# One core, an mLSTM cell into a SwiGLU block: weight pieces requested in pairs, a state sum moved, and one request placed between two halves of q's tiles

## The chip, the core and the metric

The kernel runs on one NeuronCore of one Trainium2 chip. The core has a matrix engine (TensorE, "PE" in the profile, with its weight loads as "PEld"), a vector engine (VectorE, "DVE"), a scalar engine for activations (ScalarE, "ACT"), a general engine (GpSimd, "POOL") and SyncE ("SP"), which here only issues transfers. Transfers are issued by SP and by ACT, each onto a queue of its own ("SPq", "ACTq"), and are carried out by 16 DMA engines that both queues share. Each engine runs its own instructions strictly in order, and waits on semaphores for the others.

The metric is device microseconds from start to end of one execution. The kernel before took 554.17 us (median of three runs, 553.81 to 554.72).

## What is computed

The reference has two stages. For 4 batches, 8 heads (32 sequences), 768 steps and a head width of 40, an mLSTM cell keeps a 40x40 state C, a normaliser n and a running maximum m per sequence:

```
m_new  = max(f_gate[t] + m, i_gate[t])
f_stab = exp(f_gate[t] + m - m_new);  i_stab = exp(i_gate[t] - m_new)
C = f_stab * C + i_stab * outer(v[t], k[t]);   n = f_stab * n + i_stab * k[t]
y[t] = sigmoid(o_gate[t]) * (C @ q[t]) / max(|n . q[t]|, 1)
```

The heads are put side by side, which gives x of 3072 tokens by 320, and

```
g = x @ w_gate            # 320 x 1536
h = g * sigmoid(g) * (x @ w_val)
out = h @ w_out           # 1536 x 320
```

The weights of the second stage come as float64. q, k, v and the gates are float32.

## The kernel before

**Tiling.** The 768 steps are cut into six groups of 128 tokens (`NG`), each for all 32 sequences, and each group into two chunks of 64. Within a group the cell is computed in its parallel form: scores of q and k, weights from the gates, the values weighed with them, and the state carried from chunk to chunk. The 32 sequences are handled in two halves, P = 0 and P = 1, of 16 sequences each. A group's output, 512 tokens in transposed form, then goes through the second stage in 12 blocks of 128 hidden features (`hidden(g, m)`: ten products per block, five for the gate and five for the value; the profile counts each float32 product twice, so twenty), and through w_out (`project`).

**Order.** The kernel is written out in program order by hand: what stands in the source is the order of each engine's queue. The first group has code of its own (the `first_...` functions, lines 478 to 562, called in lines 564 to 611). From then on the cell of group g+1 is computed in between the blocks of group g: `slots[m]` is a list of calls that come after `hidden(0, m)`, `ahead[m]` lists the weight blocks that are converted inside it, and `after[m]` does the same for the first group's product with w_out.

**Weights.** A float64 piece is brought in as raw 32-bit words by `piece_load(p)`. Pieces 0 and 1 hold one block of 128 features of w_gate and w_val each, pieces 2 to 6 two blocks each (piece 2 holds blocks 2 and 3, piece 3 blocks 4 and 5, and so on), and pieces 7 to 9 four row blocks of w_out each (converted as blocks 12 to 17). The gate half of a piece lands on partitions 0 to 63 and is issued by SP; the value half lands on partitions 64 to 127 and is issued by ACT for pieces 0 to 4, by SP for the rest. The raw words go to a home given by the caller (`h_sb` or `wo_sb`, which are not yet in use by then, or parts of them) or to one of two `raw` buffers, which is free again when both blocks of the piece that was in it have been scaled.

A block j is converted in three steps: `scale(j)`, two activations on ACT (`top`, line 190, and `low`, line 192); `join(j)`, two VectorE instructions that put the words together (lines 199 and 200); and `rounded(j)`, an addition of the low part (line 207) on GpSimd unless an engine is given. There is one `top` buffer and there are two `low` buffers. `hidden(0, j)` cannot start before block j is rounded.

**Psum.** There are four banks under the tag "cell" and four under "gen"; each `hidden` takes two "gen" banks and frees them when ACT (line 653) and VectorE (line 654) have read them.

**Around the change.** `first_state(P)` sums k and weighed v into the state for half P (16 small products, counted as 32) and copies it out. `first_seam(P)` transposes the group's output for the second stage. `burn(n)` runs n products of a constant tile, whose result nobody reads. `weights_load`, `weights_sub`, `weights_mask` and `weights_exp` make the weights of the next group (`w_sb`) from row maxima that pass through DRAM (`M_dram`); `weigh_values` makes `vw_sb` from them, which `do_add` needs. `load_squares` brings q's tiles of 32 by 32 with 16 small requests, eight for each parity of the head.

**Lanes.** Transfers share eight semaphores in turn, so each request waits until the request eight before it has landed.

Of the kernel before, what the change touches and what calls it, by code (L numbers as in the profile page):

```python
# [13 lines left out]
AF = mybir.ActivationFunctionType  # L14
# [10 lines left out]
def kernel(  # L25
# [18 lines left out]
    nc = tc.nc  # L44
# [7 lines left out]
    D1 = D + 1  # L52
# [4 lines left out]
    NKC = DM // HP  # L57
    UH = BH // 2
    UA = UH // 2
    NH = NFC + 1  # L60
# [15 lines left out]
    def bank(name, tag="cell"):  # L76
        return psum.tile([128, 512], F32, name=name, tag=tag)

    def half(i):
        return slice(i * SUB, (i + 1) * SUB)  # L80
# [5 lines left out]
    def heads(P):  # L86
        return slice(P * UH, (P + 1) * UH)

    k_sb = const.tile([128, BH, DP], F32)
    q_sb = const.tile([128, BH, DP], F32)  # L90
# [10 lines left out]
    wo_sb = const.tile([128, NFC, DM], F32)  # L101
    h_sb = const.tile([128, NH, TW], F32)
# [16 lines left out]
    def copy(eng, dst, src):  # L119
        if eng is nc.scalar:  # L120
            nc.scalar.copy(dst, src)
        else:
            eng.tensor_copy(dst, src)
# [16 lines left out]
    def piece_load(p, home=None):  # L140
        kind, m, n = PIECES[p]
        if kind == "gv":
            a, d = NKC, n * 128
            src = [(slice(i * HP, (i + 1) * HP), w[:, m * 128:(m + n) * 128].rearrange("(c p) f -> p c f", p=HP))
                   for i, w in enumerate((moe_w_gate, moe_w_val))]
            queues = (nc.sync, nc.scalar if p < 5 else nc.sync)
        else:
            a, d = n, DM
            src = [(slice(0, 128), moe_w_out[m * 128:(m + n) * 128].rearrange("(a p) d -> p a d", p=128))]
            queues = (nc.sync,)  # L150
        if src[0][1].dtype == F32:
            for r, w in src:
                if kind == "o":
                    nc.sync.dma_start(out=wo_sb[r, m:m + n, :], in_=w)
                else:
                    for x in range(n):
                        nc.sync.dma_start(out=wgv_sb[r, m + x], in_=w[:, :, ts(x, 128)])
            return
        if home is None:
            raw = conv.tile([128, 4 * NKC * 128], U32, name="raw")  # L160
        else:
            raw = home.rearrange("p a t -> p (a t)").bitcast(U32)
        raw = raw[:, 0:2 * a * d]
        for (r, w), queue in zip(src, queues):
            queue.dma_start(out=raw[r].rearrange("p (a d) -> p a d", a=a), in_=w.bitcast(U32))
        words = raw.rearrange("p (a d two) -> p a d two", two=2, a=a)
        raws[p] = (words[:, :, :, 0], words[:, :, :, 1])
        split(p)
# [35 lines left out]
    def rounded(j, eng=None):  # L204
        if j in blocks:
            lo, dst = blocks.pop(j)
            (eng or nc.gpsimd).tensor_tensor(dst, dst, lo, op=ALU.add)  # L207

    def convert(j, eng=None):
        scale(j)  # L210
        join(j)
        rounded(j, eng)
# [10 lines left out]
    warm = early.tile([128, 1], F32)  # L223
# [35 lines left out]
    step1 = keep1  # L259
# [46 lines left out]

    SQ = 32

    def load_squares(dst, a, c):
        for two in range(2):  # L310
            for s in range(2):
                r = slice((2 * two + s) * SQ, (2 * two + s + 1) * SQ)
                w = min(SQ, D - s * SQ)
                for t in range(L // SQ):
                    nc.sync.dma_start(out=dst[r, :, t, 0:w],
                                      in_=a[:, two:H:2, ds(c * L + t * SQ, SQ), ds(s * SQ, w)].rearrange("b h p d -> p (b h) d"))
# [6 lines left out]
    q_sq = q_sb.rearrange("p (a x) d -> p a (x d)", x=2).rearrange("p a (t d) -> p a t d", d=SQ)  # L323
# [17 lines left out]
        eng.tensor_tensor(vw_sb[:, heads(P)], v_sb[:, heads(P)], w_sb[:, heads(P), last].to_broadcast([128, UH, D1]),  # L341
                          op=ALU.mult)

    def small(name, n=UA):
        return bank(name)[:, 0:n * D1].rearrange("p (a d) -> p a d", d=D1)

    def add(n, P):
        ps = [small("add") for _ in range(2)]
# [8 lines left out]
    def state(s):  # L357
        return C_ring[s % 3]
# [103 lines left out]
    def sig(P):  # L462
        nc.scalar.activation(o_sb[:, heads(P)], o_sb[:, heads(P)], AF.Sigmoid)


    def burn(n, tag="cell"):
        t = bank("burn", tag)
        for _ in range(n):
            nc.tensor.matmul(t, lhsT=junk[:, 0:128], rhs=junk, start=True, stop=True)
# [4 lines left out]
    A, V, G = nc.scalar, nc.vector, nc.gpsimd  # L474
# [52 lines left out]
    def first_own(u):  # L527
        first_y[u] = bank("first_y", "gen")[:, 0:H * D1].rearrange("p (h d) -> p h d", d=D1)
        for h in range(H):
            nc.tensor.matmul(first_y[u][:, h, :], lhsT=W0[:, u * H + h, :], rhs=v_sb[:, u * H + h, :], start=True, stop=True)  # L530
# [13 lines left out]
            nc.vector.tensor_tensor(x, x, o_sb[:, u * H:(u + 1) * H], op=ALU.mult)  # L544
        nc.gpsimd.tensor_copy(x_sb[:, 2 * P:2 * P + 2, DM:], x_sb[:, 2 * P:2 * P + 2, 0:HP])

    def first_state(P, eng):
        ps = small("add")
        for a in range(UA):
            for two in range(2):  # L550
                h = P * UH + 2 * a + two
                nc.tensor.matmul(ps[half(two), a, :], lhsT=k_sb[:, h, :], rhs=vw_sb[:, h, :], start=True, stop=True)
        copy(eng, state(2)[:, P * UA:(P + 1) * UA], ps)

    def first_seam(P, engs):
# [30 lines left out]
    first_scores(1)  # L586
    first_x(1)
    sig(0)
    sig(1)
    piece_load(2, h_sb[:, NH - NKC:])  # L590
    piece_load(3, wo_sb)
    burn(3)
    first_own(2)
    first_own(3)
    first_gate(0)
    first_x(2)
# [1 line left out]
    first_seam(0, (A, A, V))  # L598
    scale(0)
    first_gate(1)  # L600
    burn(6, "gen")
    piece_load(4)
    join(0)
    first_seam(1, (A, A, V))
    rounded(0, V)
    first_state(0, A)
    late_decay()
    convert(1)
    nc.scalar.activation(step1, step1, AF.Exp)
    piece_load(5)  # L610
    nc.sync.dma_start(out=M_dram, in_=flat(M_sb))

# [104 lines left out]
    def load_all(dst, a, n):  # L717
        for P in range(2):
            load(dst, a, n, P)

    run = lambda f, *a: (lambda: f(*a))


    on_vector = (9, 10, 11)
    ahead = {m: [m + 2] for m in range(4)}
    ahead.update({4: [6], 5: [7, 8], 6: [9], 7: [10], 8: [11], 9: [], 10: [], 11: []})
    slots = {
        0: [run(first_state, 1, A), run(load_all, k_sb, k, 1), run(load_all, q_sb, q, 1)],
        1: [run(piece_load, 6, h_sb[:, NH - NKC:]), run(decay_rows)],
        2: [run(late_turns), run(weights_load, 1), run(load_all, v_sb, v, 1)],  # L730
        3: [run(decay)],
        5: [run(turn, 0, (A, A), (A, V))],
        6: [run(turn, 1, (A, A), (A, V)), run(weights_sub, 1, 0), run(weights_mask, 0), run(piece_load, 7)],
        7: [run(weights_sub, 1, 1), run(weights_mask, 1), run(nc.gpsimd.memset, q_sb, 0.0)],
        8: [run(weights_exp, 0), run(weights_exp, 1), run(weigh_values, G, 0), run(weigh_values, G, 1),
            run(piece_load, 8)],
        9: [run(do_scores), run(do_weigh, 0), run(do_weigh, 1), run(do_decayed, 2), run(load_all, o_sb, o_gate, 1)],
        10: [run(do_add, 1), run(do_state, 2), run(rounded, 12), run(load_squares, q_sq, q, 2)],
        11: [run(do_attend, 1, 0), run(do_gather, 1, 0, False), run(piece_load, 9)],
    }  # L740
    for m in range(NFC):
        first = [run(convert, j, V if j in on_vector else None) for j in ahead[m]]
# [34 lines left out]
    for g in range(1, NG):  # L777
        n, f = g + 1, g + 2
# [67 lines left out]
```

## Time and profile before

| | us |
|---|---|
| median of three runs | 554.17 (553.81 to 554.72) |
| the profiled execution | 555.16 |
| its span, first to last instruction | 553.0 |
| PE busy | 546.4 |
| DVE busy | 234.4 |
| ACT busy | 134.7 |
| POOL busy | 106.6 |

The span is the time from the first to the last instruction of the profiled execution; the 2.16 us beside it lie around it. All points in time given below are microseconds from the start of this span. In a timeline, a row gives the start, the duration of the whole run of like instructions, the engine, the line, and in brackets how long the engine was idle before and what ended that. The chain of waits is followed back from the last instruction: each row is what released the next one. In a table of stretches, the three numbers at the end are the granted TensorE clock (1.00 is full), the busy share of the DMA engines and the GB/s that they moved. A run of products has its end modelled, so that a row's start to the next row's start is the better measure of what it occupies.

### The profile page before, as it was taken

The numbers are of one execution on the slowest core, as the hardware profiler recorded it, in microseconds if no ns is written. First come the engines' busy times: TensorE is split into PE (matmuls) and PEld (weight loads), VectorE is DVE, ScalarE is ACT, GpSimd is POOL, SyncE is SP. The second block draws the span as 40 slices with busy tenths as digits, with TensorE's granted clock in tenths as the row PEclk, the third lists the DMA queues.
The fourth block names the chain that finished last, engine by engine and source line by source line (L and its number), as shares of the span: only waits on it lengthen the run. The fifth ranks groups of instructions, "written<-read, shape, count | busy, mean of one in ns | idle before, by whom it ended". The sixth has DMA issues, their size and how long they took to land.

```text
span 553.0 us, 11595 instructions
## 1 busy us (share of the span) xinstructions
PE 546.4 (99%) x4992; PEld 312.9 (57%) x4992; DVE 234.4 (42%) x394; ACT 134.7 (24%) x202; POOL 106.6 (19%) x97
## 2 busy tenths in 40 slices
PE   8999999999999999999999999999999999999997
PEld 4955546675545575544576455466455567444475
DVE  5956687962156332445521445531426621011100
ACT  4366564443101033110124101005110100111100
POOL 2314355574011151011133001114001200000000
PEclk9999999999999999999999999999999999999999
DMA  9999996798631763660464451395000131000000
GB/s 125 177 280 187 192 274 115 155 111 125 68 49 17 108 109 83 71 76 5 82 127 104 53 68 27 49 149 107 13 1 2 29 62 43 12 1 0 2 24 24
DMA packets 223994, 45.69 MB, mean 83 GB/s; under 512 B 214504, under 2 KB 219112, under 8 KB 223944
## 3 DMA queue, kind: packets, MB, share of 16 engines
q1 hardware_dynamic: 222036, 42.11, 46.7%
q10 hardware_dynamic: 1908, 2.85, 2.0%
q8 instruction: 39, 0.64, 0.5%
q14 instruction: 11, 0.09, 0.1%
HBM read 35.68 MB, written 4.01 MB: 72 GB/s over the span
## 4 chain that ended last, share of the span: by engine, by line
PE 92%; DMA 4%; SPq 3%; POOL 0%; DVE 0%; ACT 0%; issue 0%; ACTq 0%; POOLq 0%
PE gv_ps L648 55%; PE o_ps L664 24%; PE o_ps L671 5%; SPq L117 3%; DMA h_sb<-in_moe_w_val_dram 2%; PE inter L377 2%; PE sp L331 2%; PE intra L382 2%; DMA o_sb<-in_o_gate_dram 2%; PE add L353 1%; PE tp_kq L296 0%; POOL wgv_sb L207 0%; PE tp_x L439 0%; DVE wgv_sb L200 0%; ACT top L190 0%
## 5 line engine op out<-in xcount | busy, mean ns | idle before, releaser
L648 PE MATMUL gv_ps<-xT,wgv_sb 64*128 64x512 f32 x1440 | 317.3, 593 | 1.6 <-POOL wgv_sb L207 1.1
L648 PEld LDWEIGHTS gv_ps<-xT,wgv_sb 64*128 64x128 f32 x1440 | 139.1, 187 | 159.4 <-issue 154.6
L654 DVE TENSOR_TENSOR h_sb<-sg,gv_ps 128x512 f32<-128x512 f32 x72 | 49.5, 687 | 214.5 <-ACT sg L653 214.4
L664 PE MATMUL o_ps<-wo_sb,h_sb 128*128 128x320 f32 x480 | 130.5, 433 | 0.0
L664 PEld LDWEIGHTS o_ps<-wo_sb,h_sb 128*128 128x128 f32 x480 | 90.8, 190 | 41.0 <-issue 3.8
L653 ACT ACTIVATE sg<-gv_ps 128x512 f32<-128x512 f32 x72 | 43.0, 597 | 268.6 <-PE gv_ps L648 268.5
L362 POOL TENSOR_TENSOR C<-C,dec 128x328 f32<-128x328 f32 x20 | 14.5, 735 | 137.7 <-DVE C L369 137.6
L456 POOL TENSOR_SCALAR_AFFINE_SELECT w_sb<-w_sb 64x1024 f32<-64x1024 f32 x20 | 27.8, 1388 | 60.2 <-DVE w_sb L451 59.3
L658 ACT COPY z_sb<-o_ps 128x320 f32<-128x320 f32 x24 | 10.0, 422 | 94.7 <-PE o_ps L664 90.9
L403 POOL TENSOR_TENSOR o_sb<-o_sb,y_sb 128x640 f32<-128x640 f32 x10 | 14.3, 1428 | 79.2 <-DVE y_sb L394 79.1
L671 PE MATMUL o_ps<-wo_sb,h_sb 128*128 128x320 f32 x96 | 26.9, 437 | 0.0
L451 DVE TENSOR_TENSOR w_sb<-g_T,w_sb 128x1024 f32<-128x1024 f32 x10 | 13.2, 1355 | 27.6 <-DMA w_sb<-M_dram 27.6
L426 DVE STREAM_TRANSPOSE xT<-x_sq 128x640 f32<-128x640 f32 x16 | 12.5, 822 | 23.7 <-DMA x_sq<-x_sb 23.7
L671 PEld LDWEIGHTS o_ps<-wo_sb,h_sb 128*128 128x128 f32 x96 | 17.9, 190 | 7.2
L394 DVE TENSOR_TENSOR y_sb<-y_sb,intra 64x328 f32<-64x328 f32 x40 | 19.7, 493 | 0.8 <-PE intra L382 0.2
L369 DVE TENSOR_TENSOR C<-C,add 40x328 f32<-40x328 f32 (+1 forms) x36 | 17.7, 493 | 1.3 <-PE add L353 0.4
L207 POOL TENSOR_TENSOR wgv_sb<-wgv_sb,low 128x640 int32<-128x640 int32 x8 | 12.3, 1541 | 23.7 <-DVE wgv_sb L200 21.9
L377 PEld LDWEIGHTS inter<-C,qT 64*64 64x64 f32 x640 | 10.2, 134 | 7.3 <-issue 6.1
L341 POOL TENSOR_TENSOR vw_sb<-v_sb,w_sb 128x656 f32<-128x656 f32 x10 | 12.8, 1303 | 0.4
L338 DVE TENSOR_TENSOR w_sb<-sp,w_sb 128x512 f32<-128x512 f32 x20 | 12.7, 682 | 0.0
L460 ACT ACTIVATE w_sb<-w_sb 128x1024 f32<-128x1024 f32 x10 | 10.6, 1058 | 8.8 <-POOL w_sb L456 8.8
L397 DVE TENSOR_SCALAR den<-den 128x16 f32<-128x16 f32 x10 | 12.2, 1216 | 0.3
(129 smaller groups left out, 343.7 us busy)
## 6 DMA issues: line engine op xcount, KB each, us to landing
w_sb<-M_dram SPq DMA_DIRECT2D x10, 512.0 KB, 7.2
x_sq<-x_sb SPq DMA_DIRECT2D x128, 40.0 KB, 2.0
k_sb<-in_k_dram SPq DMA_DIRECT2D x12, 320.0 KB, 6.1
v_sb<-in_v_dram SPq DMA_DIRECT2D x12, 320.0 KB, 5.7
o_sb<-in_o_gate_dram SPq DMA_DIRECT2D x12, 320.0 KB, 5.4
raw<-in_moe_w_out_dram SPq DMA_DIRECT2D x3, 1280.0 KB, 7.8
out_dram<-z_sb SPq DMA_DIRECT2D x24, 160.0 KB, 1.8
q_sb<-in_q_dram SPq DMA_DIRECT2D x32, 64.0 KB, 2.4
```

The costliest lines, as they stand in the source:

```text
L117: nc.sync.dma_start(out=dst[:, heads(P), 0:D], in_=tokens(a, c, P))
L362: nc.gpsimd.tensor_tensor(state(s + 1)[:, a], state(s)[:, a], dec[:, s - 2, a].unsqueeze(2).to_broadcast([128, UA, D1]), op=ALU.mult)
L369: nc.vector.tensor_tensor(c, c, ps[r], op=ALU.add)
L377: nc.tensor.matmul(inter[two][half(i), a, :], lhsT=qT[half(two), P * UA + a, half(i)], rhs=state(2 * n + i)[half(two), P * UA + a, :], sta ...
L394: nc.vector.tensor_tensor(t, t, intra[i][half(c)], op=ALU.add)
L403: eng.tensor_tensor(o, o, y[:, :, 0:D], op=ALU.mult)
L456: nc.gpsimd.affine_select(w, w, compare_op=ALU.is_ge, fill=NEG, base=0, pattern=[[0, UH], [1, SUB]], channel_multiplier=-1)
L648: nc.tensor.matmul(ps[i], lhsT=wgv_sb[half(i), m, PAIRS[kc][i] if g < 2 else kc, :], rhs=x[half(i), kc, :], start=(kc == 0), stop=(kc == N ...
L653: nc.scalar.activation(sg, ps[0], AF.Silu)
L654: nc.vector.tensor_tensor(hid(g, m), sg, ps[1], op=ALU.mult)
L664: nc.tensor.matmul(p, lhsT=hid(g, m)[:, ts(u, L)], rhs=wo_sb[:, m, :], start=(m == 0), stop=(m == NFC - 1))
L671: nc.tensor.matmul(ps[u], lhsT=hid(g, m)[:, ts(u, L)], rhs=wo_sb[:, m, :], start=(m == 0), stop=(m == NFC - 1))
```

## The change

It has these parts:

- Piece 2's raw words go to `h_sb[:, 1:6]` instead of `h_sb[:, 8:13]`. That place still holds the first group's weights `W0` of sequences 4 to 23 until `first_own(2)` has read them, so the request stands after `first_own(2)` in the source, on both queues. On ACT it stands between the sigmoids of the two halves (`sig(0)`, `sig(1)`).
- Piece 3 goes to `h_sb[:, 8:13]` instead of `wo_sb` and is requested after the first `first_seam`; piece 4 goes to `wo_sb` instead of a `raw` buffer and is requested after block 1 is converted; piece 6 goes to a `raw` buffer instead of `h_sb`.
- `first_state` is split: the products of half 1 are moved from the slot after block 0 to the place of five of the six constant products before the second `first_seam`, in a "gen" bank; its copy is moved from ACT to VectorE (`first_kept`).
- Blocks 1 and 2 are rounded by VectorE instead of GpSimd. Block 2 is converted in the slot after block 0, instead of inside it.
- ACT runs a Silu on one column ahead of the first block; the exponential of `step1` moves from ahead of block 0 to the slot after block 1.
- Both subtractions and masks of `w_sb` stand in the slot after block 7 (before: one each after blocks 6 and 7).
- The last piece of w_out (piece 9) is requested between the two parities of q's tiles instead of after all of them.

```diff
@@ -306,8 +306,8 @@
 
     SQ = 32
 
-    def load_squares(dst, a, c):
-        for two in range(2):
+    def load_squares(dst, a, c, both=(0, 1)):
+        for two in both:
             for s in range(2):
                 r = slice((2 * two + s) * SQ, (2 * two + s + 1) * SQ)
                 w = min(SQ, D - s * SQ)
@@ -341,8 +341,8 @@
         eng.tensor_tensor(vw_sb[:, heads(P)], v_sb[:, heads(P)], w_sb[:, heads(P), last].to_broadcast([128, UH, D1]),
                           op=ALU.mult)
 
-    def small(name, n=UA):
-        return bank(name)[:, 0:n * D1].rearrange("p (a d) -> p a d", d=D1)
+    def small(name, n=UA, tag="cell"):
+        return bank(name, tag)[:, 0:n * D1].rearrange("p (a d) -> p a d", d=D1)
 
     def add(n, P):
         ps = [small("add") for _ in range(2)]
@@ -544,12 +544,15 @@
             nc.vector.tensor_tensor(x, x, o_sb[:, u * H:(u + 1) * H], op=ALU.mult)
         nc.gpsimd.tensor_copy(x_sb[:, 2 * P:2 * P + 2, DM:], x_sb[:, 2 * P:2 * P + 2, 0:HP])
 
-    def first_state(P, eng):
-        ps = small("add")
+    def first_state(P, tag="cell"):
+        ps = small("add", tag=tag)
         for a in range(UA):
             for two in range(2):
                 h = P * UH + 2 * a + two
                 nc.tensor.matmul(ps[half(two), a, :], lhsT=k_sb[:, h, :], rhs=vw_sb[:, h, :], start=True, stop=True)
+        return ps
+
+    def first_kept(P, ps, eng):
         copy(eng, state(2)[:, P * UA:(P + 1) * UA], ps)
 
     def first_seam(P, engs):
@@ -586,11 +589,10 @@
     first_scores(1)
     first_x(1)
     sig(0)
-    sig(1)
-    piece_load(2, h_sb[:, NH - NKC:])
-    piece_load(3, wo_sb)
     burn(3)
     first_own(2)
+    piece_load(2, h_sb[:, 1:1 + NKC])
+    sig(1)
     first_own(3)
     first_gate(0)
     first_x(2)
@@ -598,15 +600,18 @@
     first_seam(0, (A, A, V))
     scale(0)
     first_gate(1)
-    burn(6, "gen")
-    piece_load(4)
+    ps1 = first_state(1, "gen")
+    burn(1, "gen")
+    piece_load(3, h_sb[:, NH - NKC:])
     join(0)
     first_seam(1, (A, A, V))
     rounded(0, V)
-    first_state(0, A)
+    first_kept(0, first_state(0), A)
+    first_kept(1, ps1, V)
     late_decay()
-    convert(1)
-    nc.scalar.activation(step1, step1, AF.Exp)
+    convert(1, V)
+    nc.scalar.activation(warm, warm, AF.Silu)
+    piece_load(4, wo_sb)
     piece_load(5)
     nc.sync.dma_start(out=M_dram, in_=flat(M_sb))
 
@@ -723,20 +728,22 @@
 
     on_vector = (9, 10, 11)
     ahead = {m: [m + 2] for m in range(4)}
+    ahead[0] = []
     ahead.update({4: [6], 5: [7, 8], 6: [9], 7: [10], 8: [11], 9: [], 10: [], 11: []})
     slots = {
-        0: [run(first_state, 1, A), run(load_all, k_sb, k, 1), run(load_all, q_sb, q, 1)],
-        1: [run(piece_load, 6, h_sb[:, NH - NKC:]), run(decay_rows)],
+        0: [run(convert, 2, V), run(load_all, k_sb, k, 1), run(load_all, q_sb, q, 1)],
+        1: [run(piece_load, 6), run(nc.scalar.activation, step1, step1, AF.Exp), run(decay_rows)],
         2: [run(late_turns), run(weights_load, 1), run(load_all, v_sb, v, 1)],
         3: [run(decay)],
         5: [run(turn, 0, (A, A), (A, V))],
-        6: [run(turn, 1, (A, A), (A, V)), run(weights_sub, 1, 0), run(weights_mask, 0), run(piece_load, 7)],
-        7: [run(weights_sub, 1, 1), run(weights_mask, 1), run(nc.gpsimd.memset, q_sb, 0.0)],
+        6: [run(turn, 1, (A, A), (A, V)), run(piece_load, 7)],
+        7: [run(weights_sub, 1, 0), run(weights_mask, 0), run(weights_sub, 1, 1), run(weights_mask, 1), run(nc.gpsimd.memset, q_sb, 0.0)],
         8: [run(weights_exp, 0), run(weights_exp, 1), run(weigh_values, G, 0), run(weigh_values, G, 1),
             run(piece_load, 8)],
         9: [run(do_scores), run(do_weigh, 0), run(do_weigh, 1), run(do_decayed, 2), run(load_all, o_sb, o_gate, 1)],
-        10: [run(do_add, 1), run(do_state, 2), run(rounded, 12), run(load_squares, q_sq, q, 2)],
-        11: [run(do_attend, 1, 0), run(do_gather, 1, 0, False), run(piece_load, 9)],
+        10: [run(do_add, 1), run(do_state, 2), run(rounded, 12), run(load_squares, q_sq, q, 2, (0,))],
+        11: [run(do_attend, 1, 0), run(do_gather, 1, 0, False), run(piece_load, 9),
+             run(load_squares, q_sq, q, 2, (1,))],
     }
     for m in range(NFC):
         first = [run(convert, j, V if j in on_vector else None) for j in ahead[m]]
```

## The prediction

> **What bounds the kernel now.** I read the page first, then the chain of waits in order of time, then the timelines of PE, ACT and VectorE around the one place where the chain leaves PE, and last the rates of the transfers there.
>
> ```profile
> PE 546.4 (99%) x4992; PEld 312.9 (57%) x4992; DVE 234.4 (42%) x394; ACT 134.7 (24%) x202; POOL 106.6 (19%) x97
> PE 92%; DMA 4%; SPq 3%; POOL 0%; DVE 0%; ACT 0%; issue 0%; ACTq 0%; POOLq 0%
> ```
>
> PE is the bound; the 8% of the chain that is not PE lies at the start. The chain of waits shows where it ends:
>
> ```profile
> 25.43 13.59 DMA h_sb<-in_moe_w_val_dram
> ...
> 39.17 0.81 ACT top L190
> ...
> 40.01 0.51 DVE wgv_sb L199
> ...
> 41.51 1.54 POOL wgv_sb L207
> ...
> 43.10 4.80 PE gv_ps L648 x20
> 47.90 0.74 PE tp_g L622 x10
> ...
> 68.70 12.93 PE gv_ps L648 x60
> ```
>
> From 43.10 to the end PE hardly waits (one gap of 0.33 at 100.65). So what counts is when block 2 ends (47.90) and whether everything behind it can follow. Until then block 2 waits for piece 2's value half, requested at 25.43 and landed at 39.02. Three blocks in a row cost 12.93, 4.31 each. PE's timeline:
>
> ```profile
> 27.50 1.46 PE L469 MATMUL burn<-junk 128*128 128x512 bf16 x6
> 28.79 1.52 PE L561 MATMUL tp_x<-ident,x_sb 128*128 128x128 f32 x10
> 30.24 1.13 PE L552 MATMUL add<-vw_sb,k_sb 128*64 128x41 f32 x32
> 31.90 4.56 PE L648 MATMUL gv_ps<-xT,wgv_sb 64*128 64x512 f32 x20 [0.53 <-DVE m_in L285]
> 36.39 1.13 PE L552 MATMUL add<-vw_sb,k_sb 128*64 128x41 f32 x32
> 37.45 4.56 PE L648 MATMUL gv_ps<-xT,wgv_sb 64*128 64x512 f32 x20
> 43.10 4.80 PE L648 MATMUL gv_ps<-xT,wgv_sb 64*128 64x512 f32 x20 [1.08 <-POOL wgv_sb L207]
> ```
>
> Blocks 0 to 2 take 31.90 to 47.90, 16.0 us, where three in a row would take 12.93: half 1's state products lie between (37.45 - 36.39 = 1.06), then the gap, and block 2 itself is long because its second bank is freed only at 43.29, when VectorE has read block 0 (its row starts at 42.60, behind the Silu that ACT reaches at 41.97 after scaling block 2).
>
> **The change, part by part.**
>
> Products. Five of six constant products go (1.46 / 6 = 0.24 each); half 1's 1.06 comes in: 27.50 + 1.06 + 0.24 = 28.80, where the next transposes started at 28.79, released by VectorE's gating. Nothing gained or lost there (bounds: -0.1 and +0.1). Block 0 then starts at 31.90 as before: it waits for its rounding on VectorE, row 30.94 plus 0.82. Between blocks 0 and 1 the 1.06 goes.
>
> Block 1's weights. VectorE does, from 31.76, the copy of half 1's state (0.43 on ACT before), late decay (1.05 in three rows), join (0.49 and 0.83) and rounding (0.82): 35.5. Needed at 31.90 + 4.31 = 36.21. Covered by 0.7; if the cover is gone PE waits by the excess.
>
> Block 2's weights. ACT reads block 0 at about 36.25 (0.60), then `top` 36.75 to 37.55; VectorE multiplies block 0 until 37.6, joins until 38.95, rounds on VectorE until 39.9 (0.82 instead of POOL's 1.54). Needed at 31.90 + 8.62 = 40.52. Cover 0.6, if piece 2 is in. From landing to block 2's start it took 43.10 - 39.02 = 4.1, now 3.4 with the faster rounding, so the latest harmless landing is 37.1.
>
> When does piece 2 land? Both halves now wait for `first_own(2)` on PE (half of a run from 22.88 to 26.54, so 24.7). The gate half is 1.8 later than its 22.94, the value half 0.7 earlier than its 25.43. On ACT the wait holds up only the second sigmoid, which waited until 25.42 for o_gate anyway. Before, the gate half took 10.4 to land (33.3) and the value half 13.6. Ends: 24.7 + 10.4 = 35.1 and 24.7 + 13.6 = 38.3. I take 35.1, nearest the gate half's row, because of the rates:
>
> ```profile
> 30.00:32.00 2.00, 1.47 (x37) 1.22 (x36) 1.97 (x6) 1.32 (x5) 0.00 (x0) 1.00 1.06 196
> 38.00:40.00 2.00, 2.00 (x12) 0.96 (x10) 0.00 (x0) 0.82 (x2) 0.00 (x0) 1.00 1.07 360
> ```
>
> At 30 us the SP queue alone runs, with the gate half; at 38 us both queues run, one filling each half of the partitions: 196 against 360 GB/s at the same busy share. The value half could not be slowed by its partner. [...]
>
> ACT. The `step1` exponential (0.74) moves behind block 1's Silu, with one more table load (1.28, rows of 33.48 and 40.67): ACT is then done with block 1 at 41.2, exponential 43.2, block 4's scaling 44.7, Silu table 46.0; block 2's Silu runs 1.1 late, but its banks are needed only by block 4 at about 50. The state turn that reads `step1` stands after block 2 (44.8). Zero. Without cover the delay itself would be paid, at most 2.8.
>
> Pieces 3 and 4. Their value halves are now issued at about 30.0 and 35.6 (after block 0's and block 1's scaling on ACT) instead of 26.07 and 30.04. With the longest times to landing that such requests had (16.7 and 18.1) they are in at 46.7 and 53.7, with 10.4 at 40.4 and 46. Block 4 is scaled from 43.2 on ACT and due at 50.5 on PE; at 46.7 its rounding ends at 50.6. Block 6 is scaled at 51 and due at 60.8. Nothing, at worst 0.1.
>
> Blocks 1 and 2 leave POOL (2 x 1.54), which was idle there. Zero.
>
> Queues. SP: pieces 2, 3, 4 and 5 come earlier or at the same time, M's write and k's reload keep their order behind them. In the DMA engines, the bytes of pieces 2 to 5 took from 28 to 47.5, of which about 8 us (gate half of 2, value half of 5) at the one-queue rate; now the one-queue stretches are piece 4's and 5's, a little less. So `w_sb` still lands at about 71.0 (bounds 69 and 72). Piece 6, in a `raw` buffer, waits for block 1's scaling, long done. Piece 8 waits for block 11's scaling (about 72.8; before it was issued at 72.25): zero, block 14 needs it after 92.
>
> `w_sb`'s subtractions. VectorE used to stand 1.31 waiting for `w_sb` at 70.97, with block 7's product behind it. Now block 7's product goes first (about 71.3), then 1.22 and 1.21; POOL's masks 3.01 each until 78.5, memset 1.80, values 2.57: 82.9. The sum that needs them stood at 88.08 and is now due at 85.0. Cover 2.1.
>
> Piece 9 between the halves of q's tiles waits for block 13's scaling (90 before, so 87 now); eight small requests wait behind it on SP, then `w_sb`'s reload, which itself waited for PE until 101.7. Their row of 16 lasts 10.3, so eight end by 93. Zero; q's transposes come at 120.
>
> Sum: 47.90 - (31.90 + 12.93) = 3.07 earlier for block 2's end and everything behind. The profiled execution took 555.16 (553.0 span and 2.16 around it), 0.99 over the median; 552.1 against it, and 554.17 - 3.07 = 551.1 against the median.
>
> **The rivals.** (1) Piece 2 still lands late. For: it must wait for PE now, and its gate half is requested later. Against: the rates. Each microsecond after 37.1 costs one: at the old 39.0 block 2 starts at 42.4 and costs 4.49, gain 1.0, time 553.2; nothing is left at 40.0. (2) The gain is given back behind block 2, at `w_sb`: its chain is 11.9 from landing to values, so with 2.1 of cover a landing 2.1 after 71.0 begins to cost, and one at 76 gives all back (554.2). Against: fewer one-queue bytes stand ahead of it. Half given back: 552.6. (3) Slower: the constant products kept PE's clock up, and without five of them it drops in block 0. Price: at half clock a block takes 4.31 more, so one slow block gives 551.1 + 4.3 = 555.4, and 0.7 of a block turns the sign. Against: the granted clock is 1.00 in every row, also between 10 and 22 us where no constant products ran, and PE's place is filled with other products.
>
> **How the numbers follow.** All in line: 0.62, 550.5 to 551.6 (0.33 at 100.65 may go, 0.5 for cover that is too thin). Rival 1: 0.17, 551.6 to 553.6. Rival 2: 0.11, 552 to 554.6. Rival 3: 0.10, 555.3 and over. 550.5 to 553.4 holds about 0.82. About 0.2% (1.1 us) is what a measurement of this kernel can tell from no change. Under 553.06: 0.62 + 0.13 + 0.04 = 0.79; within: 0.11; over 555.28: 0.10.
>
> **What would show it.** Right: blocks 0, 1 and 2 in one run of some 12.9 from 31.9, no 1.08 gap; piece 2's halves landing together by 37; the state turn (L627 then) at 44.8; block 11 and the sums about 3 earlier. Wrong: a gap ahead of block 2 released by VectorE (rival 1), ahead of the L353 sums (rival 2), or a clock under 1.00 (rival 3); or block 0 starting after 31.9, because piece 0 now shares the DMA engines with piece 2's value half, which I price at nothing.

## The result, and the profile after

The changed kernel took 553.06 us (median of 13 executions, 551.14 to 553.55); the kernel before took 554.72 beside it (13 executions, 552.73 to 557.46). The ratio is 0.996, 95% interval 0.9948 to 0.9972: faster by 0.4%, 1.7 us, where 3.07 had been forecast.

The 13 times fall into two groups that do not overlap. Six lie at 551.14 to 552.00 (median 551.69), and their mean granted clock is 1.000. Seven lie at 553.06 to 553.55 (median 553.32), and theirs is 0.997. At half clock for 3.41 us the mean over 551 us is 1 - 0.5 x 3.41 / 551 = 0.997. So the seven hold one such stretch, and it costs 1.63 us. The profile that was kept (553.2 us, span 551.2) is one of the seven.

First the busy times and the chain's shares on the page of the changed kernel:

```profile
PE 546.0 (99%) x4985; PEld 317.7 (58%) x4987; DVE 235.5 (43%) x397; ACT 135.9 (25%) x203; POOL 104.3 (19%) x95
PE 98%; DVE 1%; ACT 0%; issue 0%; ACTq 0%; DVEq 0%
```

The 7% of the chain that was a transfer and its queue is gone. The chain in order of time (start, us, what) shows how:

```profile
27.05 2.19 PE tp_x L564 x10
...
32.52 0.82 DVE wgv_sb L207
33.34 0.14 issue
33.48 13.15 PE gv_ps L653 x60
46.62 0.74 PE tp_g L627 x10
47.36 4.49 PE gv_ps L653 x20
```

Blocks 0 to 2 are one run of 13.15 (12.93 forecast), with neither the state products between them nor the gap of 1.08. But the run begins at 33.48, not at 31.90, so block 2 ends at 46.62 instead of the forecast 44.83. The windows of PE say why; their columns are the stretch, its length, PE's busy time, the granted clock, the DMA share and GB/s:

```profile
24.00:26.00 2.00, 2.00 (x20) 1.00 1.15 218
26.00:28.00 2.00, 2.00 (x15) 0.69 1.16 198
28.00:30.00 2.00, 2.00 (x22) 0.50 1.07 201
30.00:32.00 2.00, 1.84 (x32) 0.96 1.06 217
32.00:34.00 2.00, 1.73 (x37) 1.00 1.05 239
34.00:36.00 2.00, 2.00 (x12) 1.00 1.04 304
36.00:38.00 2.00, 2.00 (x12) 1.00 1.04 358
```

The clock is 0.5 from 26.76 to 30.17, while PE turns half 0's x (2.37 in the timeline, 1.29 in the profile of e_mid below, at full clock) and sums half 1's state (1.58, 1.13 before the change). The GB/s column shows a second thing: the 300 GB/s at which both halves of a piece move together begins only at 34. Piece 2's halves were both requested at 25.26. The gate half landed at 32.6. The value half's first packet moves at 30.3, 5.0 after the request, and that half landed at 37.6.

### The profile page after: what moved, and what is told of

It reads as the page before. It is cut to its first block, busy times and chain, and to the rows that moved or that the text cites. A ratio compares the mean times of both kernels' runs of the same rounds, so it can differ in the third digit from the quotient of the medians.

```text
span 551.2 us, 11585 instructions
## 1 busy us (share of the span) xinstructions
PE 546.0 (99%) x4985; PEld 317.7 (58%) x4987; DVE 235.5 (43%) x397; ACT 135.9 (25%) x203; POOL 104.3 (19%) x95
## 4 chain that ended last, share of the span: by engine, by line
PE 98%; DVE 1%; ACT 0%; issue 0%; ACTq 0%; DVEq 0%
PE gv_ps L653 57%; PE o_ps L669 24%; PE o_ps L676 5%; PE inter L377 2%; PE sp L331 2%; PE intra L382 2%; PE add L353 1%; PE first_y L530 1%; PE burn L469 1%; PE tp_x L564 1%; PE tp_kq L509 1%; PE sp L519 1%; PE wps L480 0%; PE tp_kq L296 0%; PE wps L484 0%; PE wps L489 0%
## 5 line engine op out<-in xcount | busy, mean ns | idle before, releaser
L653 PEld LDWEIGHTS gv_ps<-xT,wgv_sb 64*128 64x128 f32 x1440 | 143.2, 187 | 154.2 <-issue 150.5
L207 POOL TENSOR_TENSOR wgv_sb<-wgv_sb,low 128x640 int32<-128x640 int32 x6 | 9.2, 1538 | 23.8 <-DVE wgv_sb L200 23.8
```

The lines of the kernel that those rows point to most:

```text
L653: nc.tensor.matmul(ps[i], lhsT=wgv_sb[half(i), m, PAIRS[kc][i] if g < 2 else kc, :], rhs=x[half(i), kc, :], start=(kc == 0), stop=(kc == N ...
```

## The experiments

Two questions were open: what halves the clock, and which parts of the change are worth what. Kernels measured together share runs of the kernel before: 555.71 us (median of 20) for the first four below, 555.17 (35) for the next four, 555.17 (35) for the last four. Against 554.72 beside the result, times of different groups can so stand up to 1 us apart for no cause in the kernel; ratios and the gaps in the profiles are read first.

### The clock

**The changed kernel again, beside the next three (r_after).**

> The changed kernel once more, for the spread of its granted clock. Theory A (stretch): TensorE's clock is halved for one window of 3.41 us whenever such a window lies wholly inside the stretch that holds only small float32 products and transposes, from the last of the three constant products (about 23.0) to the next constant product (28.9 here, 27.5 before). Then about (28.9 - 23.0 - 3.41) / 3.41 = 0.7 of the executions have a mean clock of 0.997 and take some 1.5 us more than the rest; the rest take 551.1 to 552.0. Theory B (number): the drop comes from there being five constant products fewer, wherever they stand; the same numbers here. Theory C (chance): the drop has nothing to do with the products, and the kernel before shows it as often.

Measured: 552.18 (551.66 to 553.43, 6 executions) against 555.71, ratio 0.9938 (0.9922 to 0.9954). Four executions at clock 1.000 take 551.66 to 552.44, two at 0.997 take 553.25 and 553.43: the same two groups. In its profile the clock is 0.5 from 26.54 to 29.95. Over both sets of the changed kernel 9 of 19 executions lose clock, where theory A had said 0.7 of them.

**The constant products spread out (e_mid).** The count stays; two of the three go between the products of `first_own(2)` and `first_own(3)`.

```diff
-    burn(3)
+    burn(1)
     first_own(2)
...
+    burn(2)
     first_own(3)
```

> Two of the three constant products that stand before first_own(2) are put between first_own(2) and first_own(3); all else as in the changed kernel, and the same number of products. Theory A: the stretch is cut into pieces shorter than 3.41 us, so no execution drops below 1.000; block 0 starts up to 0.35 later, because first_own(3) ends 0.5 later and VectorE had 0.2 of slack there; all executions 551.4 to 552.2. Theory B: the number is unchanged, so about half of the executions still show 0.997 and 553.2. Theory C: also about half.

Measured: 552.52 (551.15 to 552.67, 5), ratio 0.9934 (0.9918 to 0.995). None of the five lost clock, as theory A has it, where 9 of 19 executions of the changed kernel did. With that share, five without would come by chance in (10/19)^5 = 4%, so this speaks for the place of the products mattering, but does not settle it; and the median is no better than that of r_after.

**All six constant products back, half 1's state products still early (e_six).**

```diff
+    burn(6, "gen")
     ps1 = first_state(1, "gen")
-    burn(1, "gen")
```

> The changed kernel with all six constant products back, ahead of the state products of half 1. Theory A: the stretch ends at 27.5 as before, so about 0.3 of the executions drop; each takes 1.2 us more than the changed kernel at full clock, since 1.46 of constant products and 1.06 of state products no longer fit before the transposes of 28.8: 552.9 at full clock. Theory B: no execution drops; 552.9. Theory C: half drop.

Measured: 553.45 (552.41 to 555.02, 9), ratio 0.9961 (0.9946 to 0.9975). Two of nine executions still lose clock (554.64 and 554.8). At full clock (0.999 or 1.000 here and below) the median is 553.27, 1.45 over r_after, and in its profile block 0 starts at 32.66, where e_mid's has 31.57. Five products more are 1.22 (5 x 0.24). So the removed products do not keep every execution at full clock, and about their whole length lies on the path where state products fill the place.

**The kernel before with one constant product instead of six (b_one).**

```diff
-    burn(6, "gen")
+    burn(1, "gen")
```

> The kernel before with one constant product instead of six at that place, nothing else. Theory A: the stretch ends at 27.5 still (if one product counts), about 0.3 of executions drop; the time stays that of before within 0.3 us either way, because block 2 waits for piece 2, landed at 39.0, and a block 0 that starts 1.5 later is mostly hidden by that wait. Theory B: half of the executions drop, and the time is still that of before. If five products fewer made the kernel slower by themselves, this run shows it: over 555.

Measured: 555.61 (554.62 to 557.61, 12), ratio 1.0001 (0.9988 to 1.0014). Four of twelve lose clock; they take 556.35 against 555.10 for the rest, but two of them show 0.993 and 0.994, two stretches. More telling is the kernel before itself: over the three groups 44 of its 90 executions have a mean clock of 0.996 or 0.997, and they take no longer than the others (555.71 against 556.03, 555.11 against 555.18, 555.25 against 554.96). So the halved clock was there all along, as often as in the changed kernel (theory C's sign), and cost nothing that shows. That fits a stretch at the same place, hidden by the wait for piece 2. The wait was 1.08 long in the profile and the stretch costs some 1.6, so a part of it, at most 0.5, should be left over, which these medians are too coarse to show; and no profile of the kernel before fell on such an execution, so the place itself is inferred.

What decides it can be narrowed. In the 14 profiles (both kernels and the twelve), the clock first goes up to 1.00 between 3.87 and 6.57 us. In the four where it does so at 5.72 or later (5.72, 6.06, 6.28, 6.57) it is halved 20.48 later, which is six times 3.41; in the ten where it does so at 5.47 or earlier it is not halved before 100. These times fit a clock that is set on a grid of 3.41 us whose phase differs between executions; with one phase of it the clock drops after the step that ends at 26.2 to 27.05. That the grid runs on where no change of the clock shows it is an inference from these times.

The traces also show what that step holds. In the four profiles it is filled with 28 to 31 of the 32 products of `first_own(2)` and `first_own(3)` (L530, 128x41) and holds at most one of the three constant products ahead of them. In the ten others every step with more than 20 of these products also holds 1.6 to 2.8 constant products (the nearest is b_late's step from 22.54, with 26 and 1.6), and e_mid puts two constant products in their middle. So in these four the clock drops after a step with hardly anything but these products, though PE's rows there have no gap over 0.2. This is read from 14 profiles; no run set the phase.

### The parts ahead of block 2, undone one at a time

**Requests and homes of pieces 2, 3, 4 and 6 as before (u_req).**

```diff
+    sig(1)
+    piece_load(2, h_sb[:, NH - NKC:])
+    piece_load(3, wo_sb)
     burn(3)
     first_own(2)
-    piece_load(2, h_sb[:, 1:1 + NKC])
-    sig(1)
...
-    piece_load(3, h_sb[:, NH - NKC:])
+    piece_load(4)
...
-    piece_load(4, wo_sb)
...
-        1: [run(piece_load, 6), ...
+        1: [run(piece_load, 6, h_sb[:, NH - NKC:]), ...
```

> The changed kernel with the requests of pieces 2 to 4 and 6 and their homes as before the change; products, rounding and all else as changed. Theory D (requests): piece 2's value half lands at about 39.0 again, block 2 starts 3.4 later, at 42.4, so 2.0 of the 3.1 go: 553.8 on a scale where the changed kernel takes 551.8 at full clock, and a dropped clock ahead of block 0 costs nothing more, since it lies in the shadow of that wait. Rival E (requests do nothing): the value half landed at 37.7 in the changed kernel's profile, only 1.3 earlier, so the gain is that of products and rounding alone: within 0.5 of the changed kernel.

Measured: 553.28 (552.13 to 558.0, 12), ratio 0.9963 (0.9938 to 0.9988). At full clock (5 executions) the median is 552.19, and the seven at 0.996 or 0.997 have one of 553.48: the dropped clock was not hidden, though the expectation said that it would be.

**Half 1's state products behind block 0 again (u_state).**

```diff
-    ps1 = first_state(1, "gen")
-    burn(1, "gen")
+    burn(6, "gen")
...
-    first_kept(1, ps1, V)
...
-        0: [run(convert, 2, V), ...
+        0: [lambda: first_kept(1, first_state(1), A), run(convert, 2, V), ...
```

> The changed kernel with the state products of half 1 back behind block 0, copied by ACT, and the six constant products back in their place. Theory: PE pays 1.06 for the products and about 0.2 for starting block 1 anew, unless the time is covered by a wait for piece 2, which is not there: 1.2 over the changed kernel at full clock, about 553.0. Rival: block 2's weights are late anyway, and the products fill that wait: no difference.

Measured: 553.47 (552.84 to 556.88, 12), ratio 0.9978 (0.9963 to 0.9993); 553.21 at full clock.

**Blocks 1 and 2 rounded by GpSimd (u_pool).**

```diff
-    convert(1, V)
+    convert(1)
...
-        0: [run(convert, 2, V), ...
+        0: [run(convert, 2), ...
```

> The changed kernel with blocks 1 and 2 rounded by GpSimd as before. Rounding takes 0.7 longer in each. By the prediction block 2 had 0.6 of cover at full clock, so 0.1 to 0.3 slower (552.0); with no cover at all, 0.7 to 1.0 slower.

Measured: 553.39 (552.47 to 554.56, 12), ratio 0.9963 (0.9949 to 0.9977); 553.0 at full clock.

PE's timelines of the three (start, us, line, operation; in brackets the idle time before and what ended it), first with the requests as before:

```profile
31.96 8.85 PE L653 MATMUL gv_ps<-xT,wgv_sb 64*128 64x512 f32 x40 [0.28 <-DVE wgv_sb L207]
41.68 4.56 PE L653 MATMUL gv_ps<-xT,wgv_sb 64*128 64x512 f32 x20 [0.87 <-DVE wgv_sb L207]
```

with the state products behind block 0:

```profile
31.74 4.56 PE L651 MATMUL gv_ps<-xT,wgv_sb 64*128 64x512 f32 x20 [0.28 <-DVE m_in L285]
36.23 1.13 PE L552 MATMUL add<-vw_sb,k_sb 128*64 128x41 f32 x32
37.30 8.85 PE L651 MATMUL gv_ps<-xT,wgv_sb 64*128 64x512 f32 x40
```

and with GpSimd's rounding:

```profile
31.72 8.85 PE L653 MATMUL gv_ps<-xT,wgv_sb 64*128 64x512 f32 x40 [0.28 <-DVE wgv_sb L207]
41.15 4.56 PE L653 MATMUL gv_ps<-xT,wgv_sb 64*128 64x512 f32 x20 [0.58 <-POOL wgv_sb L207]
```

All three are profiles at full clock, and in all of them block 0 starts within 0.1 of the forecast 31.90 or earlier. Each undone part puts one stretch back in front of block 2: 0.87 for the requests, 1.07 for the state products (37.30 - 36.23), 0.58 for the rounding. GpSimd's rounding is only 0.72 slower (1.54 against 0.82), so block 2's cover with VectorE's is about 0.72 - 0.58 = 0.14. The times at full clock, 0.4, 1.4 and 1.2 over r_after, do not tell such amounts apart, since groups stand up to 1 apart. Of the expectations, the 1.2 for the state products is near the row; the 2.0 for the requests was too much, and the 0.1 to 0.3 for the rounding too little.

The 0.87 of the requests has a closer cause. In the traces a landing shows as sixteen updates of a semaphore (in the kernel before's, 704 for the 44 requests on each of six semaphores, 693 on two). For piece 2's value half, fifteen of them come by 36.82 and the last at 38.33 in u_req; in the kernel before by 37.63 and at 39.02; in u_sq, a run with the changed requests described below, by 36.67 and at 37.28. So block 2 waits for the last of the sixteen, which lags by 1.5 and 1.4. What holds it back was not tried.

### The late part

**The order of the late slots as before (u_late).** The subtractions and masks of `w_sb`'s first pair go back behind block 6, and all sixteen requests for q's tiles ahead of piece 9.

```diff
-        6: [run(turn, 1, (A, A), (A, V)), run(piece_load, 7)],
-        7: [run(weights_sub, 1, 0), run(weights_mask, 0), run(weights_sub, 1, 1), ...
+        6: [run(turn, 1, (A, A), (A, V)), run(weights_sub, 1, 0), run(weights_mask, 0), run(piece_load, 7)],
+        7: [run(weights_sub, 1, 1), ...
...
-             run(load_squares, q_sq, q, 2, (0,))],
-        11: [..., run(piece_load, 9), run(load_squares, q_sq, q, 2, (1,))],
+             run(load_squares, q_sq, q, 2)],
+        11: [..., run(piece_load, 9)],
```

> The changed kernel with the first subtraction and mask of w_sb back behind block 6, and all of q's tiles ahead of the last piece of w_out. Theory: nothing, within 0.3 us. Rival: the wait of VectorE for w_sb (landing near 70) comes back ahead of block 7's product, now that block 6 ends 3 us earlier, and holds up PE: up to 1 us slower.

Measured: 556.31 (555.3 to 559.08, 12), ratio 1.0028 (1.0013 to 1.0043). The expectation was nothing, or up to 1. Without these two moves, both priced at zero, the kernel is slower than the one before. Its PE timeline has a gap that no releaser explains:

```profile
98.27 1.14 PE L377 MATMUL inter<-C,qT 64*64 64x41 f32 x64
99.22 0.78 PE L382 MATMUL intra<-v_sb,w_sb 64*64 64x41 f32 x40
102.22 0.88 PE L382 MATMUL intra<-v_sb,w_sb 64*64 64x41 f32 x24 [2.21 <-issue]
```

and its windows show what ran until then, and what followed (columns as above):

```profile
96.00:98.00 2.00, 2.00 (x8) 1.00 0.95 303
98.00:100.00 2.00, 2.00 (x106) 1.00 0.85 335
100.00:102.00 2.00, 0.00 (x1) 1.00 0.03 7
102.00:104.00 2.00, 1.78 (x26) 0.54 0.04 12
104.00:106.00 2.00, 2.00 (x6) 0.61 0.64 148
```

PE stands in the middle of a group of like products that wait for nothing, just after piece 9's 1.31 MB have moved at over 300 GB/s. That points to the program itself. The page of the changed kernel lists a queue for it:

```profile
q8 instruction: 39, 0.64, 0.5%
```

39 transfers of 16 KB. PE has 4985 products and 4987 weight loads, and 9972 instructions in 39 transfers of 0.64 MB in all come to 256 a transfer and 64 bytes each: an estimate from these counts, which fits queue 8 being TensorE's program. In this profile one of its transfers starts at 99.55, as piece 9's packets (95.5 on) thin out, and PE goes on 2.67 later. Hence theory P (the transfer of program waits behind piece 9's) against S (the subtractions made the loss), and four kernels.

**Only the requests undone (u_sq).**

> The changed kernel with all sixteen requests for q's tiles ahead of piece 9, as in the kernel before; the subtractions stay late. Theory P (program page): TensorE's program is fetched in transfers of 16 KB of its own, and the one it asks for near 95 us waits behind piece 9's packets. Piece 9 is then asked for near 94, its packets run from 95 to about 99.7, the page's packet starts at about 99.5 and TensorE stands from about 99.4 to 102: a gap of about 2.5 in the row of L382 (intra), time 551.9 + 2.5 = 554.4, and up to 556.1 where the granted clock is halved for 3.41 us after it. Theory S (the subtractions of w_sb made the loss when the late part was undone): no gap, the time of the changed kernel, about 552.

Measured: 554.71 (551.14 to 556.98, 12), ratio 0.9982 (0.9956 to 1.0009), in groups far apart. Six executions at clock 1.000 have a median of 552.18 (five of them 551.14 to 552.45, the sixth 554.55, the time that P has for a gap alone), five at 0.994 (two halved stretches) lie at 556.80 to 556.98, and one at 0.997 takes 554.87. The profile is one at clock 1.000, and has no gap:

```profile
96.23 1.14 PE L377 MATMUL inter<-C,qT 64*64 64x41 f32 x64
97.18 1.13 PE L382 MATMUL intra<-v_sb,w_sb 64*64 64x41 f32 x64
98.24 6.19 PE L676 MATMUL o_ps<-wo_sb,h_sb 128*128 128x320 f32 x22
```

Here PE is early enough: its transfer of program starts at 94.28, before piece 9's first packet at 94.97. So the order of the requests is a race. An execution that loses 1.6 at 27 would come too late for it, and then pay the gap and a second halved stretch as well, 4.7 in all. That the slow executions have the gap is argued from their time and clock; none of them was profiled.

**Only the subtractions undone (u_sub).**

> The changed kernel with the subtractions and masks of w_sb's first pair back behind block 6; piece 9 stays between the halves of q's tiles. Theory P: no gap at L382; only the 0.45 by which the run of blocks 7 to 9 was longer (13.55 against 13.10 in the profile of the kernel with the whole late part undone), so about 552.3. Theory S: most of the 4 us lost there, about 555.

Measured: 554.33 (553.29 to 557.46, 12), ratio 0.9979 (0.9963 to 0.9995); 553.89 at full clock. There is no gap at L382, as P has it, but the cost is about 2 and not the 0.45 that I wrote. VectorE's timeline:

```profile
71.41 1.23 DVE L451 TENSOR_TENSOR w_sb<-g_T,w_sb 128x1024 f32<-128x1024 f32 x1 [3.21 <-DMA w_sb<-M_dram]
...
78.56 1.64 DVE L200 SCALAR_TENSOR_TENSOR wgv_sb<-top,wgv_sb 128x640 uint32<-128x640 uint32 x1
80.33 1.54 DVE L207 CUSTOM_DVE_ANT_0 wgv_sb<-wgv_sb,low 128x1280 uint16<-128x1280 uint16 x1
```

It stands 3.21 for `w_sb` (1.31 in the kernel before), with the conversion of the next weight blocks behind it, and PE needs 81.53 - 67.08 = 14.45 for the three blocks ahead of the next scores (L331) instead of 80.29 - 67.26 = 13.03. So 1.42 of the 2 has its place; the rest lies within what groups differ by.

**All sixteen requests first, and piece 9 behind the next load of `w_sb` (u_p9).**

```diff
-        11: [..., run(piece_load, 9), run(load_squares, q_sq, q, 2, (1,))],
+        11: [...],
...
-        1: [run(do_gather, 1, 1), run(weights_load, 2), run(load_all, v_sb, v, 2)],
+        1: [run(do_gather, 1, 1), run(weights_load, 2), run(piece_load, 9), run(load_all, v_sb, v, 2)],
```

> All sixteen requests for q's tiles first, and piece 9 only behind the load of w_sb for the next step (asked for near 103, landing near 108.5; its first block is scaled near 113). Theory P: nothing stands before the program page asked for near 95, its packet starts at about 96, no gap at L382, the time of the changed kernel (about 552). Rival Q (the sixteen requests in a row, or what they collide with, hold TensorE up, not piece 9's packets): the gap of about 2.5 stays, 554.4 or more. If piece 9 is too late for its blocks, a new wait near 113 to 118 in o_ps (L676) shows it.

Measured: 556.21 (554.59 to 557.15, 12), ratio 1.0014 (0.9999 to 1.0029). The gap at L382 is gone although all sixteen requests stand in a row, which speaks for P and against rival Q (one profile, in which PE was early too). The time is lost elsewhere, at the place that the expectation named with the wrong due time: block 16 is scaled at 104.88 in u_sq, not near 113. ACT waits 10.09 for piece 9 with the copies of xT queued behind it (L121), PE waits for these, and the clock is halved from 113.31:

```profile
109.47 0.78 ACT L190 ACTIVATE top<-raw 128x640 f32<-128x640 f32 x1 [10.09 <-DMA raw<-in_moe_w_out_dram]
...
110.83 0.73 ACT L121 COPY xT<-tp_x 128x512 f32<-128x512 f32 x2
```

```profile
111.45 1.37 PE L439 MATMUL tp_x<-ident,x_sb 64*128 64x64 f32 x20 [1.40 <-ACT xT L121]
```

**The kernel before with the late part alone (b_late).** Its diff is the change's in `load_squares` and in the slots 6, 7, 10 and 11.

> The kernel before with the late part alone: subtractions of w_sb behind block 7, piece 9 between the halves of q's tiles. Theory P: it takes away only the gap at L382 of the kernel before, 0.33 in one profile and 1.5 in that of the kernel with a single constant product, so 0.3 to 1.5 faster, 553.7 to 554.9 where the kernel before takes 555.2. If the late part is worth the same 4 us in either kernel: about 551.2.

Measured: 555.02 (552.96 to 556.88, 12) against 555.17, ratio 0.9983 (0.9963 to 1.0003). The gap at L382 is gone in its profile, but the 0.3 to 1.5 that P forecast cannot be told from nothing in the times. In the kernel before, the late part is worth little or nothing that can be told; in the changed kernel it is worth 4.

P also shows in where PE stops. The kernel before, and the same with five constant products fewer (b_one), have these rows:

```profile
99.89 0.75 PE L382 MATMUL intra<-v_sb,w_sb 64*64 64x41 f32 x34
100.98 0.67 PE L382 MATMUL intra<-v_sb,w_sb 64*64 64x41 f32 x30 [0.33 <-issue]
```

```profile
98.97 0.77 PE L382 MATMUL intra<-v_sb,w_sb 64*64 64x41 f32 x39
101.00 0.56 PE L382 MATMUL intra<-v_sb,w_sb 64*64 64x41 f32 x25 [1.26 <-issue]
```

With five products fewer ahead, PE stops five products later in the group, and in u_late, which has five fewer too, after 40. Counted from the start, it stops after 1106, 1106 and 1107 recorded products. A stop at a fixed place in the count is what the end of a piece of program would give; a wait for data would stay with its product.

The profiles agree in one table, which counts from the first o_ps product (one of h with w_out) as a mark. PE runs dry 4.1 after it when the transfer is late (100.65 - 96.59, 99.74 - 95.67, 100.00 - 95.92), and goes on 2.4 to 2.7 after the transfer starts:

| kernel | first o_ps product | transfer of program starts | later by | gap at L382 |
|---|---|---|---|---|
| only the requests undone (u_sq) | 93.88 | 94.28 | 0.40 | none |
| before, late part alone (b_late) | 96.78 | 97.69 | 0.91 | none |
| changed | 95.32 | 96.32 | 1.00 | none |
| before | 96.59 | 98.34 | 1.75 | 0.33 |
| before, one constant product (b_one) | 95.67 | 98.61 | 2.94 | 1.26 |
| late part undone (u_late) | 95.92 | 99.55 | 3.63 | 2.21 |

The other eight profiles lie at 0.59 to 1.29 and have no gap there either. In the last three rows piece 9's packets were still running 1.3 after the mark (95% of them had started by 98.12, 98.73 and 99.46), and the transfer starts as they end. That it waited for them is inferred from this order, and two runs bear it out, u_p9, which takes the packets away from this place, and b_late, where piece 9 lands at 97.44 instead of 99.48: neither has the gap. The two profiles of b_one and the kernel before fit too: PE came 0.92 earlier to this place, and lost 0.93 more there.

## Why the prediction was right, and where it was not

- **What bounds the kernel, and what ends block 2.** Right. With the three early parts the gap and the products between the blocks go, and each part put back brings its own stretch back.
- **The sum, 3.07.** Right at full clock, 554.72 - 551.69 = 3.0. The median, 553.06, lies in the range of 550.5 to 553.4, but outside the likeliest case, 550.5 to 551.6, and 2.0 over its point. Against the kernel before beside it, 1.7 came of the 3.07. One term did it, block 0's start: I took 31.90 "as before"; at half clock it is 33.48. At full clock it starts at 31.57 (e_mid) to 32.05 (u_sq), so the prediction's own reason for a late start, shared DMA engines, is not what showed. That the range still held is partly luck: its upper part was there for a late piece 2, and the loss came from the clock.
- **Rival 3, the clock.** What failed was the reason against it: "the granted clock is 1.00 in every row" was true of one execution, and nearly half of the others of that same kernel (44 of 90, by a mean of 0.996 or 0.997) had a halved stretch, hidden, as far as is known, by the wait for piece 2. The mechanism is not the one named: it begins at 26.2 to 27.05, ahead of the place of the removed products, and with them back two of nine executions still lose clock. Its price was 1.63, not 4.31, because it lasts 3.41, of which half is lost, and not a whole block.
- **Rival 1, piece 2's landing.** Forecast 35.1 to 38.3, taken at 35.1; the value half landed at 37.6, and in the profiles of e_mid and u_sq, at full clock, at 36.7 and 37.3. The limit of 37.1 was nearly exact: in u_sq VectorE ends block 2's rounding at 39.71 + 0.83 = 40.54, and PE wants it at 32.05 + 8.62 = 40.67. Reading 360 GB/s as what both halves do together was right; that they would start together, and that the partner could not slow the value half, was not: it moved nothing for 5.0 us after its request.
- **Block 2's cover.** Forecast 0.6 "if piece 2 is in"; about 0.1 is left. In u_sq ACT has read block 0 at 36.61 + 0.60 = 37.21, where I had 36.75, and then stands 0.18 for piece 2. So the faster rounding on VectorE, which the forecast used as 3.4 instead of 4.1, is needed almost whole, 0.58 of its 0.72.
- **Half 1's state and the constant products.** Right: 1.07 gone between the blocks, nothing added; with all six products back, 1.45 in time and 1.1 in block 0's start.
- **The moves of `w_sb` and piece 9, "zero".** Right as costs: in the changed kernel VectorE subtracts from 73.04 on without a wait, and PE has no gap up to the sums at 86.88. Wrong as an account. At full clock the changed kernel takes 551.82 (r_after), with the subtractions put back 553.89, with the requests 552.18, with both 556.02. The subtractions are what carries the gain past `w_sb`, whose landing did not come earlier. The requests are what carries it past the program transfer. By these numbers the two together are worth more than their sum (4.2 against 2.4), as if the 2 lost to the first made PE late for the second; but the 556.02 is the middle of three executions, and over all executions the medians simply add up (2.15 and 2.53 against 4.13). The gap of 0.33 at 100.65, which I noted without asking for its cause, was the only sign of it in the profile before.

## What to carry to other kernels

When a bound engine is made earlier, look behind the place for every transfer that will not come earlier with it, and price the moves that make room for it as part of the gain: alone they may be worth nothing, and without them the gain may be lost. Ask for the cause of a small gap "ended by issue" in a long unrolled stream: here one of 2.21 at L382 (u_late) is absent in u_sub, where only the place of a request of 1.31 MB differs, which fits the engine's own program held up by that transfer. So there the place of a large transfer is worth trying. And read the granted clock of many executions: here a mean of 0.996 or 0.997 in 44 of 90 of the kernel before cost nothing that shows, and in the changed kernel, without the wait of 1.08, one of 0.997 goes with 1.63 more.

## What the runs showed of the hardware that I had not expected

- The mean granted clock is 0.996 or 0.997, as one stretch of 3.41 us at half clock gives by the sum above, in about half of all executions of either kernel (44 of 90 before, 9 of 19 after). In the four profiles that show such a stretch ahead of block 0, it comes 20.48 after the clock's first rise.
- A stall of 2.21 us (u_late, at 100.00) was followed by another halved stretch from 102.15, and one of 1.40 (u_p9, at 110.04) by one from 113.31. Both begin a whole number of 3.41 us after the clock's first rise (28 after 6.57, 32 after 4.09), right behind the step of that grid that holds the stall. After the stall of 1.26 in b_one's profile the clock stayed at 1.00, and so it did after one of 1.65 in e_six's (129.45 to 131.10), which lies across two steps of the grid with 0.7 and 0.9 in them. So by an estimate from these, half of 3.41, a stall with such a stretch behind it costs up to 1.7 more than its length.
- By the estimate from the counts above, TensorE's program comes in 39 transfers of 16 KB on a queue (q8) that the page lists beside those of the data, and the one that started as 1.31 MB of weights ended (u_late) did so 3.63 after the mark instead of 0.4 to 1.3.
- A transfer requested on ACT's queue at 25.26 moved its first packet at 30.3, when the last packets of its partner on SP's queue were leaving; in the kernel before, requested at 25.43, at 32.5. Why it waits was not tried.
